# Eight input chunks loaded ahead of all weights in a scan and two-MoE kernel, with the second half's raw first-matmul blocks staged in the chunks' space

## The chip, the cores and the metric

The kernel runs as one program on 1 core of one Trainium2 chip. Its time is the device time of one execution in microseconds (us); lower is better. The engines are TensorE (PE; its weight loads are listed as PEld), VectorE (DVE), ScalarE (ACT), GpSimd (POOL) and SyncE (SP). SP does no arithmetic here: it issues transfers (DMAs). ACT and POOL issue transfers too, between their own instructions.

## The reference, cut to what matters

```python
def reference(x, f_logit, lower_bound, ...):        # x: (2, 5056, 256) f32
    f = lb + (1 - lb) * sigmoid(f_logit)
    h = 0
    for t in range(S):                               # per batch and channel
        h = f[:, t] * h + (1 - f[:, t]) * x[:, t]
        y[:, t] = h
    x = y.reshape(10112, 256)
    x = moe(x, logits = norm(x) @ norm(emb).T / tau, w1 (8,256,1024), w2 (8,1024,256))
    return moe(x, logits = x @ w_gate, another w1, w2)

def moe(x, logits, w1, w2):                          # top-1 of 8 experts
    e = argmax(logits); gate = softmax(logits)[e]
    return gate * (relu(x @ w1[e]) @ w2[e])
```

A gated scan runs over 10112 tokens (two sequences of 5056), and its output passes through two layers in which each token goes to one of eight experts.

## The kernel before, in words

**Chunks.** The scan works on chunks of 256 tokens, 40 of them, channels on the partitions. A chunk is one transfer of 512 KB (`p_load`, line 445) that holds x and the gate logits. Its steps are: `p_gate` (a tanh on ACT, line 452, and a scale and offset of two 128x256 halves on POOL, line 460, or on ACT, line 458), `p_scan` (on DVE one product, line 183, and two scans, line 486), `p_mm` (PE transposes to rows of tokens, line 501, and router logits, line 503), `p_sq`, `p_pow`, `p_hi` and `p_lo` (the rows are stored as a high and a low f16 part), and for each pair of chunks the routing (`p_seed` to `p_gat`, mostly small DVE instructions) and `p_put` (POOL scatters 128 rows at a time into the table X in DRAM, line 660).

**Weights.** Everything is multiplied in split f16: a weight block is loaded raw in f32 (`w_load`, line 370, 512 KB for one expert's half of one matrix), ACT makes its high part (`w_hi`, line 383), and the low part, raw minus high, is made either by one DVE instruction over 128x1024 (`w_lo`, line 395 through the helper at line 183) or by PE (`w_sub`, lines 404 and 405: four matmuls) with two ACT evacuations (`w_sub2`, line 413). `wpe` says how many of each 16 blocks take the way by PE: 4 of the first 16 and 8 of the second 16. Hidden features are cut in two halves h. Half 0 has 16 blocks (8 of W1, 8 of W2), and half 1 has 16 more. `W1[h]` and `W2[h]` hold the finished parts; the two tiles of half 1 also serve as space at the start:

- the first eight chunks are loaded into the eight expert slots of `W2[1]` (`alias`),
- the raw half-0 blocks of W1, then five raw half-0 blocks of W2, are loaded into the slots of `W1[1]` (`wal`); the last three go to a ring `ws` of three buffers,
- all raw half-1 blocks go through that ring.

A DVE low part of half 1 may be issued only after the first tile table is written (`issue_after(tablast[0])`, line 1144).

**Tables and units.** At checkpoints (after 16, 32, 48, 64 tiles of 128 tokens) DVE writes a table of full expert tiles (`checkpoint`, its last step `tab` at line 712). SP then reads tile addresses from it and issues a DMA transpose of each tile (`t_load`, line 767), and PE works on units: `mm1` (line 792, 24 matmuls), evacuation by ACT and DVE into `hT` (lines 800 and 801), and three units later `mm2` (lines 812 and 815). The first table gives nine tiles, 18 units: the first four tiles' half 0 (units 0 to 3), their half 1 (units 4 to 7), and then both halves of one tile after another. Unit 18 is the first that needs the second table, which needs chunks 8 to 15.

**Order.** All steps are put into numbered slots with a priority by hand (`at(slot, priority, function)`); the first unit is slot 0, and the slots run from -31. Up to slot 17 only SP's instructions keep exactly this order; the orders of PE, ACT, DVE and POOL are made by a scheduler that starts from the slots, with the steps of the first eight chunks named in `urgent` going first. `hwq()` issues a load from SP before slot -6 and from ACT afterwards. SP handles its issues strictly one after the other, so a load that waits for its space holds up all behind it.

Of the kernel before, what the change touches and what calls it, by code (L numbers as in the profile page):

```python
# [8 lines left out]
F32 = mybir.dt.float32  # L9
# [10 lines left out]
E = 8  # L20
# [9 lines left out]
 'lag': 3,  # L30
 'pre': 6,
 'start': -29,
 'wstep0': 1.2,
 'early': 4,
 'gact': (6, 16),
 'urgent': ('scan', 'mm', 'sq', 'pow', 'hi', 'seed', 'newton', 'top', 'rank', 'rec', 'exp', 'slot', 'up', 'gat', 'put', 'cp'),
 'gdve': 0,
 'wpe': (4, 8),
 'yg': (0, 0),
 'man0': ('SP',),  # L40
 'wa': 3,
# [20 lines left out]
 'spto': -6,  # L62
 'sc': (0, 26),
 'w1': (-8, 0.8),
 'w2': (0, 0.75),
 'w3': (0, 0.9),
 'wprio': 60,
# [55 lines left out]
def scan_moe_moe_kernel(ctx, tc, xf, emb, cst, tmp, w1a, w2a, w1b, w2b, out, seq, cfg=CFG):  # L123
# [53 lines left out]
    W2 = [wp.tile([P, E, 4, 2, D], F16, name=f"W2_{h}") for h in range(2)]  # L177
# [180 lines left out]
    def hwq():  # L358
        return SP if now[0] < cfg["spto"] else A
# [3 lines left out]
    def w_load(item):  # L363
        m, which, h, e = item
        k = 8 * which + e
        if (m, h) == (0, 0) and k < 8 + cfg["wal"]:
            t = W1[1][:, k % 8].rearrange("p k b f -> p (k b f)").bitcast(F32)
        else:
            t = st.tile([P, 1024], F32, name="ws", tag="ws")
        hwq().dma_start(out=t, in_=wsrc[m][which][:, h, e, :])  # L370
        return t
# [643 lines left out]
    for m in range(2):  # L1015
# [14 lines left out]
        for part in (tl, tails[m]):  # L1030
            for j in range(0, len(part), CT):
                d = dict(t=part[j:j + CT], at=j)
# [25 lines left out]
    def at(s, prio, fn, *a):  # L1058
        seqn[0] += 1
        slots.setdefault(s, []).append((prio, seqn[0], fn, a))  # L1060

    def first_of_all(fn):

        def run(*a):
            with tc.high_priority():
                r = fn(*a)
            return r and steps(r)

        def steps(r):
            while True:  # L1070
                with tc.high_priority():
                    if next(r, "end") == "end":
                        return
                yield

        return run
# [9 lines left out]
    first = min(s0.values())  # L1086
    for c in range(NCH):
        b = s0[c]
        PO = cfg["p"]

        def pa(name, fn, arg, b=b):
            if c < cfg["cps"][0] // CT and name in cfg["urgent"]:
                fn = first_of_all(fn)
            at(b + PO[name][0], PO[name][1], fn, arg)

        if c >= 2:
            pa("load", p_load, c)
        for name, fn in (("gate", p_gate), ("scan", p_scan), ("mm", p_mm), ("sq", p_sq), ("pow", p_pow), ("hi", p_hi), ("lo", p_lo)):
            pa(name, fn, c)
        if c % 2 or c == NCH - 1:  # L1100
            q = c // 2
            for name, fn in (("seed", p_seed), ("newton", p_newton), ("top", p_top), ("rank", p_rank), ("rec", p_rec), ("exp", p_exp), ("slot", p_slot),
                             ("up", p_up), ("gat", p_gat)):
                pa(name, fn, q)
            b, prio = s0[c] + PO["put"][0], PO["put"][1]
            if b < 0:
                at(b, prio, first_of_all(p_put) if c < cfg["cps"][0] // CT else p_put, q, range(G4))
            else:
                for j in range(G4):
                    at(b + j, prio, p_put, q, (j,))  # L1110

            def cp0(q):
                for m, cnt, n, fin, key in cpl:
                    if m == 0 and key not in xcnt and cnt <= min(NT, (q + 1) * G4):
                        checkpoint(m, n, fin, key, min(NT, (q + 1) * G4))

            pa("cp", cp0, q)


    def wseq(m, h):  # L1120
        return [(m, 0, h, e) for e in range(E)] + [(m, 1, h, e) for e in range(E)]
# [7 lines left out]
    def wstep(load, hi, lo, lo2):  # L1129
        def w_done(item):  # L1130
            assert item[0] or item[2] or now[0] <= 0, "weights too late"
            wdone.add(item)

        if lo2 in wps:
            w_sub2(lo2, *wps.pop(lo2))
            w_done(lo2)
        if lo is not None:
            t = wbuf.pop(lo)
            nlo[0] += 1
            i, k = nlo[0], (cfg["wpe"] + (0, 0))[(nlo[0] - 1) // 16]  # L1140
            if (i * k) // 16 != ((i - 1) * k) // 16:
                wps[lo] = (w_sub(lo, t), t)
            elif 16 < i <= 32 and tablast:
                with tc.issue_after(tablast[0]):
                    w_lo(lo, t)
                w_done(lo)
            else:
                w_lo(lo, t)
                w_done(lo)
        if hi is not None:  # L1150
            w_hi(hi, wbuf[hi])
        if load is not None:
            wbuf[load] = w_load(load)

    def wplan(items, start, step, ahead=0):
        x = start

        def it(k):
            return items[k] if 0 <= k < len(items) else None

        if ahead:
            for k in range(len(items)):
                at(max(first - 2, int(start + (k - ahead) * step)), cfg["wlp"], wstep, it(k), None, None, None)
        for k in range(len(items) + 4):
            at(int(x), cfg["wprio"], wstep, None if ahead else it(k), it(k - 2), it(k - 3), it(k - 4))
            x += step

    last_h0 = [i for i, u in enumerate(units) if u[0]["m"] == 0 and u[1] == 0][-1]
    last0 = [i for i, u in enumerate(units) if u[0]["m"] == 0 and u[0]["grp"] == 2][0]
    at(last0 + cfg["t0at"][0], cfg["t0at"][1], lambda: last_tiles(0))  # L1170
    wplan(wseq(0, 0), first + 1, cfg["wstep0"], cfg["wa"])
    wplan(wseq(0, 1), *cfg["w1"])
    wplan(wseq(1, 0), last_h0 + 1 + LAG + cfg["w2"][0], cfg["w2"][1] * cfg["swap"] / 16.0)
    wplan(wseq(1, 1), n1 + LAG + cfg["w3"][0], cfg["w3"][1] * cfg["swap"] / 16.0)

# [64 lines left out]
    def last_tiles(m):  # L1240
        tl = tails[m]
        if not tl:
            return
        n = nc.values_load(nums[m][0:1, 0:1], engines=ALL, min_val=0, max_val=TMAX)
        inside[0] = True
        if m:
            with tc.If(n > tl[0]["j"]):
                us = [(t, h) for t in tl for h in range(2)]
                for i in range(len(us) + 2):
                    if i < len(us):  # L1250
                        t, h = us[i]
                        if h == 0:
                            t_load(t, 0)
                            t_reg(t)
                        mm1(t, h)
                        evac(t, h)
                    if i >= 2:
                        t, h = us[i - 2]
                        mm2(t, h, h == 0, h == 1)
                        if h == 1:  # L1260
                            drain(s2(t))
            return
        with tc.If(n > tl[0]["j"]):
            kept[0] = {}
            assert ranked[1] == 0
            for d in [t["pair"] for t in tl if t["pi"] == 0]:
                for t in d["t"]:
                    t_load(t, 0, qp.tile([P, 8, TW], F16, name="xt8", tag="q")[:, 0:4, 0:P])
                    t_reg(t)
                    for h in range(2):  # L1270
                        mm1(t, h)
                        evac(t, h)
                        mm2(t, h, h == 0, h == 1)
                    drain(o_sum(t))
                    m_sq(t)
                for fn in (m_scale, m_split, m_turn, m_turn2, m_logits, m_top, m_exp, m_rank, m_gat, m_slot, m_up):
                    drain(fn(d))
                routed[0] += len(d["t"])
            kept[0] = None
        inside[0] = False  # L1280
# [128 lines left out]
```

## Time and profile before

| | |
|---|---|
| median of 3 runs | 1118.79 us (1114.92 to 1122.22) |
| the profiled execution: its own time | 1118.87 us |
| its span, first to last instruction | 1116.8 us |
| PE busy | 1027.6 us, 92% |
| DVE busy | 685.3 us, 61% |
| ACT busy | 534.3 us, 48% |
| POOL busy | 464.7 us, 42% |
| TensorE clock granted, mean | 0.964 of full speed |

The shares are means over the whole span, and the kernel has stages with different limits, so the section after the next shows the busy time by stretch. In a row, the name on the left of `<-` is the tile written and on the right what is read; a bracket at the end gives the idle time in front of an instruction and what ended it. `W` stands for any of the four weight tiles, so the first eight chunks appear as `W` and later ones as `xf`.

### The profile page before, as it was taken

The numbers are of one execution on the slowest core, as the hardware profiler recorded it, in microseconds if no ns is written. First come the engines' busy times: TensorE is split into PE (matmuls) and PEld (weight loads), VectorE is DVE, ScalarE is ACT, GpSimd is POOL, SyncE is SP. The second block draws the span as 40 slices with busy tenths as digits, with TensorE's granted clock in tenths as the row PEclk, the third lists the DMA queues.
The fourth block names the chain that finished last, engine by engine and source line by source line (L and its number), as shares of the span: only waits on it lengthen the run. The fifth ranks groups of instructions, "written<-read, shape, count | busy, mean of one in ns | idle before, by whom it ended". The sixth has DMA issues, their size and how long they took to land.

```text
span 1116.8 us, 33586 instructions
## 1 busy us (share of the span) xinstructions
PE 1027.6 (92%) x11987; PEld 813.1 (73%) x11987; DVE 685.3 (61%) x2227; ACT 534.3 (48%) x1338; POOL 464.7 (42%) x909
## 2 busy tenths in 40 slices
PE   3768899999999999798999889899999999999996
PEld 2435677888887887576877667687888888788885
DVE  8975687787778777454648987866433333333332
ACT  5877665555555554343436755544333333333332
POOL 4353555666666666522103665234222222222222
PEclk9777999999999999998999999899999999999999
DMA  9669535476754664222338739954222232232220
GB/s 356 229 188 243 137 87 110 121 130 127 141 121 116 135 133 84 72 62 47 68 50 212 186 84 215 223 87 97 62 50 49 54 54 49 46 56 43 44 49 28
DMA packets 191766, 124.14 MB, mean 111 GB/s; under 512 B 169345, under 2 KB 170254, under 8 KB 191600
## 3 DMA queue, kind: packets, MB, share of 16 engines
q1 hardware_dynamic: 167632, 49.15, 24.7%
q10 hardware_dynamic: 11344, 39.15, 12.9%
q0 software_dynamic: 12624, 33.62, 10.2%
q8 instruction: 105, 1.72, 0.7%
q14 instruction: 61, 0.50, 0.2%
HBM read 54.70 MB, written 34.66 MB: 80 GB/s over the span
## 4 chain that ended last, share of the span: by engine, by line
PE 44%; DVE 6%; DMA 2%; issue 1%; ACT 0%; POOL 0%; POOLq 0%; ACTq 0%
PE hps L792 22%; PE ops L812 15%; PE ops L815 7%; DVE W L183 1%; DMA ws<-w1b 1%; DVE trow L183 1%; DVE hT L183 1%; DVE trow L187 1%; DVE osum L191 1%; DMA X<-trow,tsl 1%; DVE ter L191 0%; DVE pi L188 0%; ACT W L383 0%; DVE tse L188 0%; PE x2p L901 0%
## 5 line engine op out<-in xcount | busy, mean ns | idle before, releaser
L792 PE MATMUL hps<-xT,W 128*128 128x128 f16 x7968 | 510.7, 220 | 13.1 <-issue 11.0
L792 PEld LDWEIGHTS <-W 128*128 x7968 | 477.8, 99 | 61.1 <-issue 20.5
L812 PE MATMUL ops<-W,hT 128*128 x1328 | 454.5, 382 | 9.2 <-ACT W L413 3.3
L183 DVE SCALAR_TENSOR_TENSOR hT<-hps,hT 128x512 f16<-128x512 f32 x332 | 228.4, 688 | 254.4 <-ACT hT L800 253.2
L815 PE MATMUL ops<-W,hT 128*128 x1328 | 364.3, 274 | 1.0 <-issue 1.0
L800 ACT ACTIVATE hT<-hps 128x512 f16<-128x512 f32 x332 | 197.5, 595 | 330.3 <-PE hps L792 262.1
L812 PEld LDWEIGHTS <-hT 128*128 128x128 f16 x1328 | 132.4, 100 | 124.8 <-issue 6.3
L1004 POOL DMA_INDIRECT out<-osum,ti x83 | 81.1, 977 | 290.8 <-DVE osum L183 256.1
L815 PEld LDWEIGHTS <-hT 128*128 128x128 f16 x1328 | 130.3, 98 | 19.8 <-issue 7.5
L984 POOL DMA_INDIRECT X<-trow,tsl x83 | 94.2, 1136 | 57.8 <-DVE tsl L191 31.9
L660 POOL DMA_INDIRECT X<-row,sl x79 | 85.1, 1077 | 52.7 <-issue 17.1
L833 ACT ACTIVATE ob<-ops,exr 128x256 f32<-128x256 f32 x83 | 39.3, 473 | 59.7 <-PE ops L815 52.8
L383 ACT ACTIVATE W<-ws 128x1024 f16<-128x1024 f32 x51 | 54.7, 1072 | 15.2 <-DMA ws<-w1b 7.7
L183 DVE SCALAR_TENSOR_TENSOR osum<-ops,exr,ob 128x256 f32<-128x256 f32 x83 | 40.2, 484 | 35.3 <-ACT ob L833 33.0
L183 DVE SCALAR_TENSOR_TENSOR W<-ws,W 128x1024 f16<-128x1024 f32 x42 | 51.1, 1218 | 9.4 <-ACT W L383 9.1
L191 POOL TENSOR_TENSOR ob<-ob,acc 128x256 f32<-128x256 f32 x25 | 23.2, 928 | 58.3 <-ACT ob L831 58.2
L858 ACT ACTIVATE trow<-osum 128x256 f16<-128x256 f32 x83 | 35.3, 425 | 23.8 <-DVE osum L191 14.9
L831 ACT ACTIVATE ob<-ops 128x256 f32<-128x256 f32 x83 | 31.3, 377 | 31.1 <-PE ops L815 15.0
L486 DVE TENSOR_TENSOR_SCAN xf<-xf 128x256 f32<-128x256 f32 (+3 forms) x64 | 42.6, 707 | 0.1
L191 DVE TENSOR_TENSOR osum<-ops,ob 128x256 f32<-128x256 f32 x83 | 34.5, 415 | 11.5 <-POOL ob L191 6.2
L183 DVE SCALAR_TENSOR_TENSOR trow<-osum,tsc,trow 128x256 f16<-128x256 f32 x83 | 39.1, 494 | 2.3 <-ACT trow L873 1.5
L873 ACT ACTIVATE trow<-osum,tsc 128x256 f16<-128x256 f32 x62 | 28.1, 501 | 20.9 <-DVE tsc L188 10.5
(165 smaller groups left out, 1142.8 us busy)
## 6 DMA issues: line engine op xcount, KB each, us to landing
xf<-xf ACTq DMA_DIRECT2D x28, 512.0 KB
ws<-w1b ACTq DMA_DIRECT2D x16, 512.0 KB
ws<-w2b ACTq DMA_DIRECT2D x16, 512.0 KB
W<-xf SPq DMA_DIRECT2D x8, 512.0 KB
W<-w1a SPq DMA_DIRECT2D x8, 512.0 KB
ws<-w2a ACTq DMA_DIRECT2D x8, 512.0 KB
xT<-X SPq DMA_TRANSPOSE x212
ws<-w1a ACTq DMA_DIRECT2D x6, 512.0 KB
```

The costliest lines, as they stand in the source:

```text
L183: return eng.scalar_tensor_tensor(out=out, in0=in0, scalar=s, in1=in1, op0=op0, op1=op1, **kw)
L191: return eng.tensor_tensor(out=out, in0=in0, in1=in1, op=op)
L383: A.activation(out=hi, in_=src, func=ACTF.Copy, scale=64.0)
L486: V.tensor_tensor_scan(out=t[:, k, lo:hi], data0=t[:, 2 + k, lo:hi], data1=t[:, k, lo:hi], initial=init, op0=ALU.mult, op1=ALU.subtract)
L660: x_write(0, G.indirect_dma_start(out=X[0], out_offset=IndirectOffsetOnAxis(ap=p["sl"][:, i, 0:1], axis=0), in_=p["row"][:, i, :].bitcast( ...
L792: T.matmul(out=hps[:, c, :], lhsT=w, rhs=xt[:, a, :], start=(n == 0), stop=(n == 5))
L800: A.activation(out=hh[:, 0], in_=hps, func=ACTF.Relu)
L812: T.matmul(out=o.rearrange("p a d -> p (a d)"), lhsT=hT[:, k, :], rhs=W2u[h][:, ds(at4[k], 4 * D)].bitcast(F16), start=(first and k == 0), ...
L815: T.matmul(out=o[:, 0, :], lhsT=hT[:, 4 + k, :], rhs=W2u[h][:, ds(at4[k], 2 * D)].bitcast(F16), start=False, stop=(last and k == 3))
L833: A.activation(out=b, in_=o[:, 1, :], func=ACTF.Copy, scale=scale)
L984: x_write(1, G.indirect_dma_start(out=X[1], out_offset=IndirectOffsetOnAxis(ap=sl[:, i, 0:1], axis=0), in_=d["row"][:, i].bitcast(I32), in ...
L1004: i = ins_of(G.indirect_dma_start(out=out, out_offset=IndirectOffsetOnAxis(ap=ti, axis=0), in_=r, in_offset=None, bounds_check=N - 1, oob_ ...
```

## The change

The eight chunks' loads are moved to the very first slots, the half-0 weights are planned ten slots after the first instead of one and follow at a denser step, the eight raw half-1 W1 blocks get loads of their own into the slots of `W2[1]` that the chunks leave, no half-1 block takes the way by PE, and the gate's scale and offset of chunks 4 and 5 go from POOL to ACT.

```diff
- 'wstep0': 1.2,
+ 'w0': 10,
+ 'wstep0': 0.85,
- 'gact': (6, 16),
+ 'gact': (4, 16),
- 'wpe': (4, 8),
+ 'wpe': (4, 0),
+ 'w1s': (20, 0.8),
...
+        elif (m, which, h) == (0, 0, 1):
+            t = W2[1][:, e].rearrange("p k b d -> p (k b d)").bitcast(F32)
         else:
             t = st.tile([P, 1024], F32, name="ws", tag="ws")
...
-        if c >= 2:
+        if 2 <= c < cfg["alias"]:
+            at(first - 2 + (c - 2) // 2, 2, p_load, c)
+        elif c >= 2:
             pa("load", p_load, c)
...
-    def wplan(items, start, step, ahead=0):
+    def wplan(items, start, step, ahead=0, staged=0):
...
-            at(int(x), cfg["wprio"], wstep, None if ahead else it(k), it(k - 2), it(k - 3), it(k - 4))
+            at(int(x), cfg["wprio"], wstep, None if ahead or k < staged else it(k), it(k - 2), it(k - 3), it(k - 4))
...
-    wplan(wseq(0, 0), first + 1, cfg["wstep0"], cfg["wa"])
-    wplan(wseq(0, 1), *cfg["w1"])
+    wplan(wseq(0, 0), first + cfg["w0"], cfg["wstep0"], cfg["wa"])
+    for e in range(E):
+        at(int(first + cfg["w1s"][0] + e * cfg["w1s"][1]), 60, wstep, (0, 0, 1, e), None, None, None)
+    wplan(wseq(0, 1), *cfg["w1"], staged=E)
```

Worked out from these numbers (`first` is -29): chunks 2 to 7 load in slots -31 to -29, where they were in -27 to -17. The 16 half-0 loads stand in slots -21 to -8, where they were in -31 to -13. The eight staged loads stand in slots -9 to -3, the first three on SP and the others on ACT's queue. The half-1 W2 loads keep their slots from -1 on.

## Rows read from the trace of the kernel before

**Rows 1.** Windows: busy time of each engine by stretch, clock, DMA share, GB/s.

```profile
core 0: us, PE busy (x) PEld busy (x) DVE busy (x) ACT busy (x) POOL busy (x), PEclk, DMA share, GB/s
0.00:9.00 9.00, 0.20 (x1) 0.10 (x1) 4.38 (x37) 2.17 (x3) 3.50 (x13) 1.00 0.81 257
9.00:35.00 26.00, 16.37 (x76) 12.36 (x76) 24.94 (x64) 18.93 (x48) 10.60 (x13) 1.00 0.83 323
35.00:50.00 15.00, 9.21 (x45) 5.99 (x46) 15.00 (x58) 15.00 (x42) 5.83 (x5) 0.66 0.83 301
50.00:62.00 12.00, 11.64 (x44) 6.43 (x43) 10.71 (x52) 9.64 (x26) 6.24 (x6) 0.57 0.44 147
62.00:73.60 11.60, 6.31 (x48) 4.33 (x45) 8.57 (x52) 8.83 (x33) 5.41 (x9) 0.87 0.81 236
73.60:89.00 15.40, 10.07 (x22) 4.59 (x21) 10.97 (x26) 9.17 (x22) 5.45 (x17) 0.61 0.78 190
89.00:109.00 20.00, 16.52 (x141) 12.30 (x139) 10.22 (x23) 14.12 (x30) 8.75 (x22) 0.78 0.97 253
109.00:135.00 26.00, 22.69 (x190) 15.31 (x189) 17.32 (x42) 17.04 (x45) 15.72 (x31) 0.93 0.70 166
135.00:157.70 22.70, 20.41 (x229) 16.34 (x228) 18.50 (x73) 13.65 (x44) 14.95 (x41) 1.00 0.28 84
...
157.70:1116.80 959.10, 914.14 (x11211) 735.36 (x11208) 564.69 (x1812) 425.71 (x1057) 388.21 (x757) 0.98 0.45 94
```

**Rows 2.** Timeline: the first and second table's last step, first and nineteenth unit.

```profile
73.39 0.23 DVE L188 TENSOR_SCALAR tab<-le,ct 128x9 int32<-128x9 f32 x1
...
157.53 0.22 DVE L188 TENSOR_SCALAR tab<-le,ct 128x16 int32<-128x16 f32 x1
...
89.04 1.91 PE L792 MATMUL hps<-xT,W 128*128 128x128 f16 x16
...
158.56 1.22 SPq L767 DMA_TRANSPOSE xT<-X  x1
...
169.21 1.50 PE L792 MATMUL hps<-xT,W 128*128 128x128 f16 x24
```

**Rows 3.** Timeline of SP's issues, and the longest wait of SP before 60 us.

```profile
18.42 13.47 SPq L370 DMA_DIRECT2D W<-w2a  x2
31.95 0.42 SPq L445 DMA_DIRECT2D W<-xf  x1
...
34.56 0.95 SPq L445 DMA_DIRECT2D xf<-xf  x2
...
SPq L370 <- PE wd L404: 12.8, 1, 12.8
```

**Rows 4.** Timeline of ACT: the tanh of chunks 0, 7 and 8.

```profile
5.52 0.63 ACT L452 ACTIVATE W<-W 128x512 f32<-128x512 f32 x1 [2.49 <-DMA W<-xf]
...
41.50 0.77 ACT L452 ACTIVATE W<-W 128x512 f32<-128x512 f32 x1
...
49.28 0.82 ACT L452 ACTIVATE xf<-xf 128x512 f32<-128x512 f32 x1
```

**Rows 5.** DVE groups by shape, 50 to 73.6 us: work of chunks 8 and later.

```profile
L183 DVE SCALAR_TENSOR_TENSOR row<-yt,sc,row 128x256 f16<-128x256 f32 x8 | 3.7, 473 | 0.4 <-ACT row L541 0.4
L486 DVE TENSOR_TENSOR_SCAN xf<-xf 128x256 f32<-128x256 f32 x4 | 2.9, 740 | 0.0
...
L183 DVE SCALAR_TENSOR_TENSOR xf<-xf 128x512 f32<-128x512 f32 x3 | 2.1, 702 | 0.1
L486 DVE TENSOR_TENSOR_SCAN xf<-xf,W 128x256 f32<-128x256 f32 x2 | 1.4, 733 | 0.0
```

**Rows 6.** DVE groups by shape, 73.6 to 157.7 us: weight low parts.

```profile
L183 DVE SCALAR_TENSOR_TENSOR W<-ws,W 128x1024 f16<-128x1024 f32 x8 | 9.7, 1219 | 4.9 <-ACT W L383 4.9
```

**Rows 7.** What DVE waited for from 73.6 to 157.7 us: total, times, longest.

```profile
DVE hT L183 <- ACT hT L800: 8.1, 6, 3.6
DVE ri L615 <- POOL ri L188: 5.1, 3, 3.2
DVE W L183 <- ACT W L383: 4.9, 4, 2.1
DVE xf L183 <- ACT xf L458: 4.2, 2, 3.0
DVE ci L183 <- PE ops L815: 1.6, 1, 1.6
```

**Rows 8.** PE groups by shape, 73.6 to 157.7 us: the way by PE.

```profile
L404 PE MATMUL wd<-ws,cs 128*128 128x512 f32 x28 | 20.4, 850 | 6.6 <-DMA ws<-w1a 6.6
...
L405 PE MATMUL wd<-W,idn 128*128 128x512 f16 x14 | 5.5, 446 | 0.0
```

**Rows 9.** ACT and POOL groups by shape: 9 to 62, 73.6 to 157.7, 0 to 62 us.

```profile
L458 ACT ACTIVATE W<-W,fb,fa 128x256 f32<-128x256 f32 x4 | 2.4, 704 | 0.0
...
L383 ACT ACTIVATE W<-ws 128x1024 f16<-128x1024 f32 x13 | 14.0, 1080 | 7.5 <-DMA ws<-w2a 4.7 <-DMA ws<-w1a 2.8
...
L413 ACT ACTIVATE W<-wd 128x512 f16<-128x512 f32 x14 | 7.9, 597 | 2.5 <-POOL rq L188 2.2 <-DVE ri L615 0.4
...
L188 POOL TENSOR_SCALAR W<-W,fa,fb 128x256 f32<-128x256 f32 x12 | 11.3, 949 | 16.6 <-ACT W L452 16.6
```

## The prediction, made before the changed kernel was run

> **What bounds the kernel now.** I read the windows first, because the shares of the whole span hide the start. From 157.7 us on PE is busy 914 of 959 us, 95% [rows 1]. The change touches no step of that part, so whatever comes earlier there moves the end by as much, and nothing else does. The lever is the head, in which PE is busy 113 of 157.7 us, part of it with weight preparation.
>
> The head has two stretches. From 9 to 50 us DVE is busy 39.9 of 41 us, 97%, while PE stands at 62% [rows 1]: DVE is the bound. From 73.6 to 157.7 us, between the two tables, DVE is busy 57.0 of 84.1 us (10.97 + 10.22 + 17.32 + 18.50), 68%; PE is busy 69.7, 83%, at a granted clock of 0.61 to 0.93 up to 135 us; ACT 54.0, 64% [rows 1]. No engine is full there; each waits for another in turn.
>
> The next view is the timeline of the tables and units. The first table ends at 73.6, the first unit starts at 89.0, the second table ends at 157.75, SP issues the transpose of unit 18 at 158.56, and PE takes that unit at 169.2 without an idle gap [rows 2]. The first unit came 15.4 us after its table, and the nineteenth came 11.5 us after its own. So PE has little slack over the second table: I estimate that it could run some 5 us ahead, and after that the second table decides. The date to forecast is that of the second table.
>
> Last, SP's own timeline. It stands in one wait of 12.8 us for a PE weight subtraction, from 18.4 to 31.6 us, since a raw W2 block wants a slot that a raw W1 block still occupies; chunk 7's load is queued behind it and issues at 31.95 [rows 3]. Chunk 0's tanh runs at 5.52, chunk 7's at 41.5 and chunk 8's at 49.3 [rows 4]. The first table needs chunk 7.
>
> **The change part by part.**
>
> Chunks first: chunks 2 to 7 are issued before any load that waits. At 323 GB/s, the rate of 9 to 35 us [rows 1], 512 KB take 1.6 us, so chunk 7 lands near 5.5 + 7 x 1.6 = 17 us, and no chunk step waits for a load. What is late next is DVE itself. Its work up to the first table was 4.38 + 24.94 + 15.00 + 10.71 + 8.57 = 63.6 us [rows 1]. Of this about 10 us belongs to chunks 8 to 10 and was only filler: scans 2.9 + 1.4, products 2.1, half of the eight row parts 1.9 [rows 5], and an estimated 1.7 of small routing steps. The other 53.6 stay: eight chunks, twelve half-0 low parts, setup, table. With 4.4 of it done by 9 us and the 97% of 9 to 50 us, taken as 96%, the table ends at 9 + 49.2 / 0.96 = 60.3 us instead of 73.6: **13.3 us earlier**. Bounds: if the scheduler puts all twelve half-0 low parts (12 x 1.22 = 14.6 us, by the mean of [rows 6]) behind the table it comes at 45, but that work then stands in the second stretch; if the order of the urgent steps stays as it is and the table still waits for its chain of small steps, it comes at 70.
>
> Half-0 weights later: eight W1 blocks of 1.6 us land behind the chunks, from 17 to about 30 us, before DVE has time for them. Nothing is lost while DVE is full. The raw W2 blocks still need the slots that these leave, so SP waits again, but now only chunks 8 and later, the W2 blocks and the three first staged loads stand behind that wait. Chunk 8's load issued at 34.56 before [rows 3] and could come 10 to 15 us later; at no cost as long as low parts fill DVE, and at up to that much idle time of DVE if they don't.
>
> Staged half-1 W1 blocks: the eight loads leave the ring of three. ACT waited 2.8 us for such blocks and 4.7 for the W2 ones [rows 9], PE 6.6 [rows 8], and DVE stood 4.9 us behind ACT's high parts [rows 7]. A staged slot is free only when its chunk's scan and transposes are over and the next chunk's scan has read its last column; for slot 7 that is chunk 8's scan. Five of the loads are issued by ACT, so ACT's evacuations and tanhs are queued behind such a wait if the order turns out wrong; I take nothing for it, and 3 us as its upper bound, the order of the single waits that these rows show.
>
> No half-1 block by PE: in the second stretch PE loses 20.4 + 5.5 = 25.9 us of busy time [rows 8] and ACT 7.9 us of evacuations [rows 9]. DVE gains eight low parts, 8 x 1.219 = 9.75 us [rows 6], all behind the first table. PE is not the bound of the table, so its 25.9 us are not a term of their own; they show in how long DVE waits.
>
> Gates of chunks 4 and 5: four POOL instructions, 4 x 0.95 = 3.8 us, become four on ACT, 4 x 0.70 = 2.8 us [rows 9]. ACT is full from 35 to 50 us [rows 1], but it loses the wait for chunk 7 and a first table at 60 leaves it slack: its 54.6 us up to 73.6 included later chunks as well. Zero, between a 2.8 us loss and, since POOL's step was in the chain of its chunk, a 1 us gain.
>
> **The sum.** Work of DVE between the tables: 57.0, plus 10 of chunks 8 to 10 that no longer stand in front of the first table, plus 9.75, minus an estimated 5.5 for scans and row parts of chunks 16 and 17 that ran before the second table without being needed: 71.2 us. Idle time of DVE there was 84.1 - 57.0 = 27.1 us. Of its causes [rows 7] the 5.1 us for POOL's small steps and 1.6 for the table's start stay. The 4.9 behind high parts should go, and the 8.1 for hT and 4.2 for gates are in part PE and ACT being held by the subtractions. There is also 20 us more work to stand in the holes. I take half, 13.5 us. The second table then ends at 60.3 + 71.2 + 13.5 = 145.0 us, 12.7 us earlier. PE can follow: it needs some 26 us less for the same units. The profiled execution took 1118.87 us, 0.1 us from the median of the runs, so 1118.87 - 12.7 = **1106 us**.
>
> The low parts go to the engine that is fullest in the head. The Trainium skill, Perfetto Trace Analysis, section Identifying the Most-Contended Engine, tells one to find the engine with the highest occupancy and to optimize it first; this edit loads that engine. By that page alone, with DVE the bound of the whole head, the time would grow. The trace agrees for 9 to 50 us and not behind the first table, where the new low parts stand. The rival it gives is the third below.
>
> **The rivals.**
>
> 1. More. If low parts and chunks keep DVE as full behind the first table as before it (7 us idle instead of 13.5) and the table comes some us earlier still, the second table ends at 60.3 + 71.2 + 7 = 138.5, 19 us earlier: 1100 us, down to 1094. For it: the work is loaded long before. Against: 5.1 + 1.6 us of waits stay, and PE and ACT get the units' work at the same time.
>
> 2. Hidden. DVE's idle time between the tables stays at 22 to 27 us, because each hT, gate and routing step still waits for another engine in turn; the earlier first table is eaten by the moved work. 60.3 + 71.2 + 22 = 153.5 gives 4 us, 27 gives 158.5: 1114 to 1120 us. For it: no engine was full in that stretch, and the total work of DVE up to the second table rises.
>
> 3. Slower, with DVE as the bound. The first table does not come earlier by what the loads allow, because DVE's chain of small steps at the end of the routing sets it and the low parts are put among them; then the 9.75 us of added low parts stand on DVE between the tables with nothing to pay for them. Second table at 157.75 + 9.75 = 167.5: 1128.6 us. It decides from the point where DVE's share between the tables falls under 71.2 / (157.75 - 60.3) = 73%, or where the first table comes later than 73.6 - 9.75 + 5.5 = 69 us with idle time as it is. For it: DVE is 97% full up to 50 us. Against: 27 us of holes behind the first table.
>
> That the change doesn't do what it says is possible only on the engines whose order the scheduler makes; it would show as rival 2.
>
> **How the numbers follow.** Forecast, 1100 to 1112: 0.45. Rival 1, below 1100: 0.15. Rival 2, 1112 to 1122: 0.25. Rival 3, above 1122: 0.15. A change of 1% is 11.2 us, about what a measurement of this kernel can tell from none, so faster means below 1107.6 and slower above 1130. Faster: all of rival 1 and some three quarters of the forecast's weight, 0.48. Slower: the upper part of rival 3, 0.10. The rest, 0.42, is within 1%. The likeliest case alone spans 1100 to 1112; the range for 8 in 10 cuts half of rival 1 and most of rival 3: 1096 to 1124.
>
> **What would show it.** SP's timeline should have chunk 7's issue before 10 us and no wait in front of it. The tanh of chunk 7 should stand before 35 us, the first table's last step near 60, the first unit near 70 to 75. Behind it, there should be 16 low parts of 1.2 us on DVE, no line 404 with half-1 blocks, and ACT's waits for raw W1 blocks gone. The second table should stand near 145 and unit 18 some 10 us behind it. From there on the distance to the end should be as before, 959 us from the second table. The prediction is wrong if the second table moves much less than the first, if ACT stalls at its staged loads, or if the part behind the second table changes its length.

## The result, and the profile after

The changed kernel takes 1110.21 us (median of 11 runs, 1107.01 to 1116.94) against 1118.79 us for the kernel before on the same chip (11 runs, 1114.92 to 1122.61): a ratio of 0.9914, 95% interval 0.989 to 0.9939. The profiled execution took 1111.67 us, its span 1109.4. The gain is 8.6 us; 12.7 were predicted, and the time lies 4.2 us above the predicted 1106.

The first view is again that of the windows, now cut at the two tables and the first unit (columns as in [rows 1]):

```profile
core 0: us, PE busy (x) PEld busy (x) DVE busy (x) ACT busy (x) POOL busy (x), PEclk, DMA share, GB/s
0.00:9.00 9.00, 0.20 (x1) 0.10 (x1) 4.20 (x36) 1.91 (x2) 3.51 (x13) 1.00 0.79 266
9.00:50.00 41.00, 27.30 (x134) 22.32 (x135) 39.76 (x139) 35.29 (x97) 12.59 (x13) 1.00 0.75 269
50.00:60.00 10.00, 3.86 (x14) 1.96 (x14) 9.04 (x57) 7.75 (x13) 6.40 (x7) 0.66 1.02 395
60.00:86.30 26.30, 13.76 (x63) 9.59 (x62) 22.48 (x43) 20.84 (x46) 17.53 (x23) 0.63 0.92 294
86.30:109.00 22.70, 18.76 (x199) 16.97 (x199) 19.53 (x51) 18.97 (x51) 13.88 (x25) 0.83 0.93 222
109.00:135.00 26.00, 22.52 (x217) 16.76 (x217) 16.11 (x52) 10.77 (x39) 18.61 (x41) 0.87 0.35 89
135.00:149.60 14.60, 11.45 (x138) 9.20 (x137) 12.56 (x60) 9.20 (x29) 8.80 (x26) 1.00 0.19 65
149.60:1109.40 959.80, 914.88 (x11184) 734.51 (x11181) 561.81 (x1805) 425.28 (x1053) 389.57 (x762) 0.98 0.45 95
```

Up to the first table DVE works 4.20 + 39.76 + 9.04 = 53.0 us. Between the tables it works 22.48 + 19.53 + 16.11 + 12.56 = 70.7 of 89.6 us, so it is idle for 18.9. Behind the second table the kernel takes 959.8 us and PE is busy 914.9 of them; before, 959.1 and 914.1 [rows 1].

The timeline of the changed kernel, with the rows that answer to [rows 2 to 4] (tanh of chunks 7 and 8; tables; first unit and units 17 and 18; SP):

```profile
21.94 0.66 ACT L456 ACTIVATE W<-W 128x512 f32<-128x512 f32 x1
53.07 0.63 ACT L456 ACTIVATE xf<-xf 128x512 f32<-128x512 f32 x1
...
59.70 0.22 DVE L190 TENSOR_SCALAR tab<-le,ct 128x9 int32<-128x9 f32 x1
149.36 0.22 DVE L190 TENSOR_SCALAR tab<-le,ct 128x16 int32<-128x16 f32 x1
...
86.33 4.90 PE L796 MATMUL hps<-xT,W 128*128 128x128 f16 x48
...
161.62 1.50 PE L796 MATMUL hps<-xT,W 128*128 128x128 f16 x24
164.31 1.50 PE L796 MATMUL hps<-xT,W 128*128 128x128 f16 x24
...
2.13 4.55 SPq L449 DMA_DIRECT2D W<-xf  x7
6.73 9.72 SPq L374 DMA_DIRECT2D W<-w1a  x8
30.48 17.19 SPq L374 DMA_DIRECT2D W<-w2a  x4
47.72 0.42 SPq L449 DMA_DIRECT2D xf<-xf  x1
...
79.31 1.30 SPq L771 DMA_TRANSPOSE xT<-X  x1
...
154.97 1.22 SPq L771 DMA_TRANSPOSE xT<-X  x1
```

The reader is to see four dates. Chunks 1 to 7 issue by 6.7 us, chunk 7's tanh runs at 21.9 instead of 41.5 [rows 4], and the first table ends at 59.9 instead of 73.6 [rows 2]. The first unit came only 2.7 us earlier, 86.3 instead of 89.0. The second table ends at 149.6, 8.2 us earlier. SP's wait moved: it stands from 16.5 to 30.5 us, and again up to 47.7, with the raw W2 blocks, and chunk 8's load, behind them, issues 13.2 us later than in [rows 3]:

```profile
SPq L374 <- PE RK L429: 11.8, 1, 11.8
SPq L374 <- DVE lg L193: 10.8, 1, 10.8
```

A count in [rows 2] is off by one. The row at 169.21 there is not the nineteenth unit; 17 evacuations into hT run on ACT before it, so it is unit 17, the eighteenth. Unit 18 follows it, in the trace of the kernel before:

```profile
171.90 1.50 PE L792 MATMUL hps<-xT,W 128*128 128x128 f16 x24
```

So unit 18 began at 171.90 before and begins at 164.31 now, 13.3 and 9.3 us behind SP's transpose for it, with no idle time of PE in front in either trace. The slack of PE over the second table was larger than the estimated 5 us.

The groups of DVE by shape from 60 us to the second table, which answer to [rows 6, 7]:

```profile
L185 DVE SCALAR_TENSOR_TENSOR W<-ws,W 128x1024 f16<-128x1024 f32 x9 | 10.8, 1214 | 0.0
L185 DVE SCALAR_TENSOR_TENSOR hT<-hps,hT 128x512 f16<-128x512 f32 x14 | 9.5, 682 | 10.3 <-ACT hT L804 8.6 <-issue 1.7
L185 DVE SCALAR_TENSOR_TENSOR W<-W,W 128x1024 f16<-128x1024 f32 x8 | 9.5, 1212 | 2.0 <-ACT W L387 2.0
```

And its waits in the same stretch:

```profile
DVE hT L185 <- ACT hT L804: 8.6, 3, 5.2
DVE xf L185 <- ACT xf L462: 2.2, 2, 1.4
DVE W L185 <- ACT W L387: 2.0, 2, 1.8
...
DVE ri L619 <- POOL ri L190: 0.5, 1, 0.5
```

Seventeen low parts stand behind the first table (the sixteen of half 1 and the last of half 0). The wait behind high parts fell from 4.9 to 2.0 us, POOL's small steps from 5.1 to 0.5. The wait for hT, 8.1 us before, stands at 8.6, of which 5.2 is one wait.

### The profile page after: what moved, and what is told of

It is laid out like the page before. It is cut to its first block, busy times and chain, and to the rows that moved or that the text cites. A ratio compares the mean times of both kernels' runs of the same rounds, so it can differ in the third digit from the quotient of the medians.

```text
span 1109.4 us, 33481 instructions
## 1 busy us (share of the span) xinstructions
PE 1012.7 (91%) x11939; PEld 811.4 (73%) x11939; DVE 685.5 (62%) x2235; ACT 530.0 (48%) x1326; POOL 470.9 (42%) x905
## 4 chain that ended last, share of the span: by engine, by line
PE 46%; DVE 5%; DMA 2%; issue 1%; ACT 1%; another core or an unknown queue 0%; POOL 0%; ACTq 0%; POOLq 0%; DVEq 0%
PE hps L796 23%; PE ops L816 15%; PE ops L819 8%; DVE W L185 2%; DMA ws<-w1b 1%; DVE hT L185 1%; DMA X<-trow,tsl 1%; PE x2p L905 1%; ACT W L387 0%; DVE osum L193 0%; DVE trow L185 0%; DVE ter L193 0%; DVE trow L189 0%; DVE acc L193 0%
## 5 line engine op out<-in xcount | busy, mean ns | idle before, releaser
L664 POOL DMA_INDIRECT X<-row,sl x79 | 91.3, 1155 | 57.2 <-ACT lg L525 23.3
L387 ACT ACTIVATE W<-ws 128x1024 f16<-128x1024 f32 x43 | 45.4, 1058 | 6.2 <-DMA ws<-w1b 5.1
L505 PE MATMUL yt<-cs,xf 128*128 128x128 f32 x126 | 28.5, 303 | 19.7 <-issue 9.2
L835 ACT ACTIVATE ob<-ops 128x256 f32<-128x256 f32 x83 | 31.4, 378 | 30.7 <-PE ops L819 15.0
```

The lines of the kernel that those rows point to most:

```text
L387: A.activation(out=hi, in_=src, func=ACTF.Copy, scale=64.0)
L664: x_write(0, G.indirect_dma_start(out=X[0], out_offset=IndirectOffsetOnAxis(ap=p["sl"][:, i, 0:1], axis=0), in_=p["row"][:, i, :].bitcast( ...
```

## The experiments

Three theories stood against each other: the order of the loads carries the gain, through the first table (A); the work that PE loses carries it (B, called D in the later expectations); the loads that no longer wait for the ring of three carry it (C). The change has three large parts, here called **order** (of the loads), **staging** (of the half-1 W1 blocks) and **low parts** (all of half 1 on DVE). The runs below hold all eight combinations. They ran on two chips, numbered 0 (the first eight runs) and 11 (the last three); each ratio is to the kernel before on its own chip (medians there 1095.05 to 1098.12 us). The result's chip has no number on record; it is taken for a third, because the kernel before took 1118.8 us on it. The times in the first four expectations are for that chip, so they are to be read as ratios to 1118.8 us.

**Order and staging, low parts left out.** The change with the second half's eight blocks back on PE.

```diff
- 'wpe': (4, 0),
+ 'wpe': (4, 8),
```

> The changed kernel with the second half's low parts shared as before: 8 of 16 by PE. Theory A (the head ends with the second table, which DVE's work and its holes set; the load order brought the first table forward): first table near 60 us as in the changed kernel, DVE between the tables loses 9.75 us of work and regains about as much in holes while PE gets 26 us back; second table 147 to 153, total 1107 to 1114. Theory B (the gain is the 26 us that PE lost; the load order is idle): second table back near 157, total 1117 to 1120.

Measured: 1090.32 us, 0.9956 (0.9924 to 0.9987). First table 59.2, second 150.9, first unit 90.1. The table dates and the ratio lie within what theory A had, the ratio at its upper edge.

**Order and low parts, staging left out.** The half-1 W1 blocks go through the ring again.

```diff
-        elif (m, which, h) == (0, 0, 1):
-            t = W2[1][:, e].rearrange("p k b d -> p (k b d)").bitcast(F32)
...
-    for e in range(E):
-        at(int(first + cfg["w1s"][0] + e * cfg["w1s"][1]), 60, wstep, (0, 0, 1, e), None, None, None)
-    wplan(wseq(0, 1), *cfg["w1"], staged=E)
+    wplan(wseq(0, 1), *cfg["w1"], staged=0)
```

> The changed kernel with the raw half-1 W1 blocks through the ring of three again instead of the chunks' slots. Theory A: first table near 60, but ACT's high parts of these blocks wait for the ring; second table 152 to 156, total 1112 to 1117. Rival (the staging is idle, since low parts may start only behind the first table and DVE has a queue anyway): 1108 to 1112.

Measured: 1090.26 us, 0.9955 (0.9933 to 0.9976). First table 58.9, second 151.7, first unit 81.3. The staging is not idle here: without it the ratio lies above that of the change (0.9846, below), with intervals apart.

**Order alone.** The kernel before with the new order of loads. Against the changed kernel it has both edits above together, and the gates of chunks 4 and 5 on POOL.

```diff
- 'gact': (4, 16),
+ 'gact': (6, 16),
- 'wpe': (4, 0),
+ 'wpe': (4, 8),
...
+    wplan(wseq(0, 1), *cfg["w1"], staged=0)
```

> Only the load order of the change (chunks first, half-0 weights later); ring, 8 of 16 by PE and the gates of chunks 4 and 5 on POOL as before. Theory A: first table 58 to 64, second table 150 to 156, total 1111 to 1117. Theory B: the first table comes early but the second stays near 157, total 1117 to 1120.

Measured: 1099.49 us, 1.003 (1.0001 to 1.0059). Theory A fell here: the first table came at 61.2, some 12 us early, and nothing was gained. The second table came at 167.0, later than either theory had it.

**Low parts alone.** The kernel before with one number changed.

```diff
- 'wpe': (4, 8),
+ 'wpe': (4, 0),
```

> The kernel before with all half-1 low parts on DVE, nothing else. Theory A: first table stays near 73, 9.75 us more work on DVE stand in 27 us of holes; second table 156 to 164, total 1117 to 1125. Theory B: PE's 26 us are the gain, second table near 149, total 1108 to 1112.

Measured: 1086.78 us, 0.9923 (0.9896 to 0.9949), as theory B had it. The second table came at 152.2. It is the largest single part, though it puts an estimated 9.75 us more (eight low parts of [rows 6]) on DVE, the fullest engine of the head.

**The change itself**, on the chip of these runs.

> The changed kernel itself, as the measure for the others on this chip: ratio to the kernel before 0.988 to 0.994, second table 8 us earlier than before.

Measured: 1080.0 us, 0.9846 (0.9806 to 0.9885), a larger gain than expected. First table 60.2, second 145.0.

**Staging alone.** The kernel before with the staged loads (the two blocks of code above, added to it).

> The kernel before with the raw half-1 W1 blocks staged in the chunks' slots, nothing else (old load order, 8 of 16 by PE). Theory C (the head's end is set by the half-1 blocks' way through the ring of three, where a block that PE takes holds its slot until PE has read it): ratio 0.990 to 0.996, second table near 151. Theory D (PE's 26 us of subtractions are what counts): ratio 0.998 to 1.003, second table near 157.

Measured: 1093.89 us, 0.9985 (0.9958 to 1.0011): not told from no change. Second table 154.0. Theory C by itself fell.

**Staging and low parts, old order.**

```diff
# the kernel before with the staged loads, and
- 'wpe': (4, 8),
+ 'wpe': (4, 0),
```

> The kernel before with staging and all half-1 low parts on DVE, but the old load order and gates. Theory A (load order carries the gain): ratio near 0.997 to 1.0. Theory C with an idle load order: 0.986 to 0.993, as good as the whole change or better by the 0.3% that the order alone lost. Theory D: the 0.992 of low parts on DVE alone.

Measured: 1089.5 us, 0.9944 (0.9926 to 0.9962), between the ranges of theories A and C; the 0.992 of theory D lies just under the interval. Without the order some 9.5 us of the gain are gone, though the order alone is worth nothing. (Its profiled execution took 1099.39 us, 10 above its median.)

**Chunks 8 and 9 earlier.** Their loads go ahead of the half-0 weights, to test whether SP's wait in front of chunk 8 costs.

```diff
+        elif 8 <= c < 10:
+            at(first + 6, 2, p_load, c)
```

> The changed kernel with the loads of chunks 8 and 9 moved ahead of the raw half-0 blocks, so that they no longer stand behind SP's 17 us wait. If DVE is full up to the first table and the late chunk 8 costs nothing: ratio to the changed kernel 0.998 to 1.002. If the late chunks make the holes behind the first table: second table 3 to 5 us earlier, ratio 0.995 to 0.997.

Measured: 1085.85 us, 0.9926 (0.9896 to 0.9955), some 6 us worse than the change, which neither expectation had. Chunk 8's tanh ran at 24.2 instead of 53, and the first table came at 64.7 and the first unit at 91.3: DVE and ACT did chunk 8's work in front of the table that doesn't need it.

**The kernel before**, for its trace on a second chip.

> The kernel before, unchanged, for its trace on this chip. If its shorter time here (1095 to 1096 us against 1118.8) lies behind the second table, as the changed kernel's traces of both chips let one think (959.8 against 937 us), then its second table stands at 155 to 160 us as in the first trace and the distance to the end is near 935. If the head is what differs, the second table comes before 145 and the distance is 950 or more.

Measured: 1096.74 us. Second table at 160.2, 934.6 us ahead of the end, so the shorter time of this chip lies behind the second table.

**Gates left on POOL.**

```diff
- 'gact': (4, 16),
+ 'gact': (6, 16),
```

> The change without its last part: the gates of chunks 4 and 5 stay on POOL. My prediction took this part as 0, between a loss of 2.8 us and a gain of 1: then the time is within 0.3% of the changed kernel's 1080.0 us (ratio to the kernel before 0.982 to 0.988), first table at 59 to 62. The rival: in the orders tried so far the load order and the gates went together or not by turns, and the gates carry what I gave to the interplay of the three edits; then this kernel falls back to a ratio of 0.993 to 0.997, as the kernels with one of the three edits missing did.

Measured: 1082.64 us, 0.9863 (0.9832 to 0.9895): inside the band for "no part". The gates of chunks 4 and 5 are worth nothing that shows, and the run without order, e3, is not spoiled by its gates.

**The change once more**, for a second trace.

> The changed kernel once more, for a second trace on one chip. If the 4.6 us between the second tables of its two traces (149.6 and 145.0) come from the chip, this one shows 144 to 146. If a profiled execution scatters by as much, it can stand anywhere from 143 to 151, and my term for the idle time of DVE can't be called off by 5 us.

Measured: 1082.67 us; second table 144.8. That is as on chip 0 (145.0), and not as on the result's (149.6), which speaks for the chip as the cause; from the result's chip there is one trace.

### What the eight combinations show together

Units run on PE in one order, so a date up to which the kernels can be compared is the end of unit 17's matmuls, where its evacuation starts. It splits into the start of the first unit and the stretch from there. The ratio is of all runs, the dates are of one profiled execution each (us). The first line's trace is from chip 11, the other seven from chip 0:

| parts | ratio | first unit | stretch to unit 17 | PE busy, idle in it | unit 17 done |
|---|---|---|---|---|---|
| none | 1 | 90.4 | 83.2 | 70.8, 12.4 | 173.6 |
| order | 1.003 | 93.0 | 87.4 | 71.2, 16.2 | 180.4 |
| staging | 0.9985 | 90.8 | 76.7 | 70.4, 6.3 | 167.5 |
| low parts | 0.9923 | 83.3 | 82.3 | 67.0, 15.3 | 165.6 |
| order, staging | 0.9956 | 90.1 | 74.2 | 68.6, 5.6 | 164.3 |
| order, low parts | 0.9955 | 81.3 | 83.8 | 65.1, 18.7 | 165.1 |
| staging, low parts | 0.9944 | 93.3 | 74.5 | 64.9, 9.6 | 167.8 |
| all three | 0.9846 | 85.8 | 70.7 | 61.6, 9.1 | 156.5 |

These dates do not add up to the ratios. From unit 17 to the end the eight traces have 916.6 to 929.8 us, though no part touches that stretch. Staging alone is 6.1 us earlier at unit 17 and gains 0.15%, some 1.6 us, by the medians. The change without its gates, as fast as the change, has its first unit at 89.5 and unit 17 at 161.0. So the ratios show which parts work together, and the dates only suggest by which way.

Each line comes from a windows view cut at those two dates. Here are those on which the reading rests, each kernel's line up to the first unit and from there. The kernel before, on the second chip:

```profile
0.00:90.40 90.40, 52.07 (x228) 33.26 (x229) 74.59 (x280) 64.03 (x164) 37.86 (x60) 0.79 0.74 249
90.40:173.60 83.20, 70.84 (x730) 53.26 (x729) 57.10 (x181) 53.88 (x143) 43.31 (x103) 0.92 0.61 148
```

Low parts alone:

```profile
0.00:83.30 83.30, 39.52 (x201) 27.28 (x201) 72.05 (x270) 59.32 (x153) 37.75 (x59) 0.77 0.73 259
83.30:165.60 82.30, 67.03 (x707) 56.06 (x708) 65.08 (x201) 50.07 (x139) 46.34 (x104) 0.84 0.69 162
```

Staging and low parts, old order:

```profile
0.00:93.30 93.30, 42.76 (x202) 29.08 (x202) 79.82 (x274) 65.15 (x158) 44.45 (x59) 0.74 0.77 274
93.30:167.80 74.50, 64.89 (x707) 54.90 (x708) 55.68 (x195) 44.08 (x134) 44.15 (x104) 0.87 0.47 121
```

Order and low parts, no staging:

```profile
0.00:81.30 81.30, 43.23 (x212) 32.92 (x213) 67.76 (x263) 58.09 (x150) 36.83 (x56) 0.88 0.73 256
81.30:165.10 83.80, 65.05 (x698) 53.20 (x699) 68.41 (x207) 53.83 (x148) 50.69 (x104) 0.85 0.63 168
```

The change, second trace:

```profile
0.00:85.70 85.70, 45.92 (x212) 33.96 (x213) 75.86 (x271) 66.53 (x159) 39.44 (x55) 0.86 0.84 288
85.70:155.90 70.20, 61.39 (x698) 50.40 (x699) 56.37 (x199) 45.47 (x136) 46.64 (x105) 0.95 0.54 139
```

Three readings follow. The first two are read from traces; the third rests on the ratios.

**Low parts on DVE free the way to the first unit.** In front of it PE's busy time falls from 52.1 to 39.5 us, and the unit comes 7.1 us earlier. The work that went is PE's own, in a stretch where its granted clock is 0.61 [rows 1]. The kernel before, on the result's chip, shows it between the first table and the first unit:

```profile
L404 PE MATMUL wd<-ws,cs 128*128 128x512 f32 x8 | 7.5, 1094 | 3.1 <-DMA ws<-w1a 3.1
...
L405 PE MATMUL wd<-W,idn 128*128 128x512 f16 x2 | 1.1, 634 | 0.0
```

That is 8.6 us of subtractions and 3.1 us of waiting for raw blocks, out of 15.4 us; the others of the same kind follow among the units. What stands just in front of the first unit differs too. In the kernel before it is a subtraction up to 89.0, and with the low parts alone it is an idle PE that waits for the transposed tile:

```profile
85.49 3.75 PE L404 MATMUL wd<-ws,cs 128*128 128x512 f32 x4 [1.23 <-DMA ws<-w1a]
...
83.33 2.08 PE L792 MATMUL hps<-xT,W 128*128 128x128 f16 x18 [2.21 <-DMA xT<-X]
```

SP issued the first transpose at 77.5 us in the one and at 77.4 in the other, so if the tile took as long to land in both, PE's own order held the unit by 5.7 us.

**Staging moves half-1 low parts from behind the first unit to ahead of it.** The windows say so: with all low parts on DVE in both, DVE's work ahead of the first unit rises from 72.0 to 79.8 us under the old order and from 67.8 to 75.9 under the new one, and in the unit stretch it falls from 65.1 to 55.7 and from 68.4 to 56.4. In low parts that is 16 without staging against 23 with it that are done before the first unit under the old order, and 15 against 22 under the new. The unit stretch gets shorter by 7.8 us under the old order and by 13.1 or 13.6 (two traces of the change) under the new one.

**The order pays for staging.** By the ratios staging is worth something on the new order alone: from 1.003 to 0.9956 without the low parts and from 0.9955 to 0.9846 with them, both with intervals apart. On the old order it gives -0.15% without the low parts and 0.2% of loss with them, neither told from nothing. How that comes about is argued from the dates. Under the old order the first unit comes 10.0 us later for that work (83.3 to 93.3, the latter in the execution that took 10 us above its median), and nothing is left of the 7.8. Under the new order the first table, and with it the chunks' part of DVE's work, is 13 us earlier, and the first unit is only 4.5 us later (81.3 to 85.8), 8.2 in the trace without the gates. The order alone has no low parts to put into that room: the half-0 weights stand later, the last weight part is finished at 146.9 instead of 139.9, and the units wait (16.2 us of idle PE against 12.4). So the single parts add up to 0.003 - 0.0015 - 0.0077, or -0.6%, and together they give -1.5%.

A larger ring, which would tell the position of the loads from the space they take, was not tried. And the dates are of one execution each, with no interval of their own.

## Why the prediction was right, and where it was off

The result is in the range and nearest to the forecast's case, 1.8 us from the edge where the second rival begins. The single likeliest outcome by the chances, faster by 1% or more (0.48), did not come; 0.86% falls within 1% (0.42). Of the prediction's signs of being wrong, the first came half true: the second table moved by 8.2 us, the first by 13.7. The others did not come: the one wait of ACT for a staged block took 2.0 us, and the part behind the second table kept its length. By the steps:

**First table**: 60.3 predicted, 59.9 measured, with 53.0 us of DVE work against 53.6. The 96% held.

**Work between the tables**: 71.2 predicted, 70.7 measured.

**Idle time between the tables**: this is the mis-sized term. "I take half, 13.5 us" met 18.9 on the result's chip, 5.4 more; with the 0.9 us that the first two terms gave back, it makes all of the miss, 149.6 instead of 145.0. By its causes it was off in both directions: the 5.1 us for POOL's small steps, which were to stay, fell to 0.5, and the 8.1 for hT, which were to go in part, stood at 8.6. The other two traces of the changed kernel have 85.0 - 71.0 = 14.0 and 84.8 - 70.2 = 14.6 us. The windows and waits of the second:

```profile
60.00:144.80 84.80, 63.97 (x610) 50.18 (x609) 70.22 (x202) 60.67 (x164) 55.59 (x112) 0.85 0.69 191
```

```profile
DVE osum L193 <- POOL ob L193: 3.4, 1, 3.4
DVE W L185 <- ACT W L387: 2.9, 2, 2.3
DVE xf L185 <- POOL xf L190: 2.7, 1, 2.7
...
DVE hT L185 <- ACT hT L804: 0.3, 1, 0.3
```

The wait for hT is 0.3 us there and 8.6 in the result's trace; an hT waits for PE to reach its unit. On the result's chip PE had a granted clock of 0.87 from 109 to 135 us and did 217 matmuls. That is a mean over both levels: from 117 to 121 us it was at 1.00 with PE busy for 2.86 of the 4 us, and from 121 to 125 us at 0.57. In this trace it had 1.00, the upper level (2.4 GHz), throughout and did 250 in the same busy time (22.5 and 22.4 us):

```profile
109.00:135.00 26.00, 22.44 (x250) 18.22 (x251) 18.16 (x63) 14.60 (x50) 20.19 (x47) 1.00 0.42 124
```

The third trace of the changed kernel has 0.93 there, 250 matmuls and a wait for hT of 1.1 us. Why the clock differs is not settled, and that it makes the wait is argued from these three traces; there is one of the changed kernel from the result's chip.

**Distance to the end**: "as before, 959 us" and 959.8 measured.

**"PE is not the bound of the table, so its 25.9 us are not a term of their own."** The first half of this sentence failed, and the sum survived it. The low parts alone are half of the change's worth on their chip, and they work through PE: the first unit 7.1 us earlier. The second half held: between the tables of that run DVE is idle for 17.1 us, against 29.2 in the kernel before on chip 11, and the second table comes 8.0 us earlier. In the result's own traces the gain up to unit 17 can be written wholly in PE's terms. Before, and then after:

```profile
89.00:170.80 81.80, 72.73 (x730) 54.87 (x729) 55.92 (x181) 53.21 (x144) 43.50 (x103) 0.92 0.60 150
```

```profile
86.30:163.20 76.90, 64.51 (x698) 52.43 (x699) 56.86 (x199) 45.67 (x140) 48.39 (x105) 0.90 0.51 125
```

The first unit is 2.7 us earlier, PE works 8.2 us less in the stretch and idles 3.3 more (12.4 for 9.1): 2.7 + 8.2 - 3.3 = 7.6 us, against 7.2 in the two profiled executions. That is a way to book the gain and not yet a proof of its cause. The second table served as a mark, since PE's order mixes the units with the chunks' transposes and logits that the table needs; it was not what unit 18 waited for. The prediction took it for the cause, and that its distance to the end stayed the same was in this sense luck. As a mark it is as good as unit 17: from the second table to the end the eleven traces of chips 0 and 11 have 930.0 to 941.3 us, from unit 17 916.6 to 929.8.

**"Half-0 weights later: nothing is lost while DVE is full."** Not so by itself: the order alone finishes its weights 7 us later and is slower by 0.3%. In the change staging and the low parts on DVE finish all weights at 109 us, and there the order gains 1.0% (0.9944 to 0.9846).

**Staging.** It was priced by the waits of ACT, PE and DVE for raw blocks (at most 4.9 + 2.8 + 4.7 + 6.6). Those fell: ACT's from 7.5 us [rows 9] to 2.4, not to zero. What the runs suggest as its worth is another thing: seven more low parts done ahead of the first unit, where the new order had made room.

**Chunk 8 later.** Foreseen as 10 to 15 us, measured 13.2. No cost of it was found: bringing it forward made the kernel slower.

**Gates.** Taken as zero; the change without them differs by less than its interval.

**First unit near 70 to 75.** Wrong: 86.3. The sixteen scatters of the first eight chunks end at 74.0, hardly ahead of the 75.6 before, because POOL's first one waits for the routing until 40.7 and two of them are slow (below); the first transpose follows at 79.3. But in the other two traces the transposes began at 73.1 and 76.6 and the first unit still came at 85.8 and 85.7. In front of it on PE stand the transposes and logits of chunks behind the table, at a clock of 0.63 from 60 to 86.3 us in the result's trace, and waits for DVE and ACT. Which of them holds it was not separated.

**The rivals.** The third needed DVE to be the bound between the tables. The run with the low parts alone is its direct test, some 9.75 us more on DVE, and it is 0.77% faster. The Trainium skill, Perfetto Trace Analysis, section Identifying the Most-Contended Engine, says to find the engine with the highest occupancy and optimize it first. In the stretch in question this trace has PE, not DVE, as the fuller engine by the time of its matmuls (83% against 68% [rows 1]), and so taken the rule agrees with the result; by the whole head it does not. But for TensorE the same section of the Trainium skill sets the matmul time aside as a measure and names, beside the arithmetic done, the busy share of the weight loads. That share is 48.5 of 84.1 us here, 58% [rows 1], less than DVE's, and so taken the rule misses the result in this stretch too.

The second rival, idle time of 22 us or more, did not come true, though 18.9 lies nearer to it than to the forecast's 13.5; the first (7 us) came true in no trace.

## What to carry to other kernels

Room that a new load order makes early in a kernel is worth nothing until other work is ready to be put into it: the order alone gave nothing (+0.3%) and staging alone nothing (-0.15%), but both together gave -0.4%, and with the lightened PE (-0.8% alone) -1.5%. So parts of a change are to be priced together where one makes room and another fills it. And a date that moves with the end is not yet its cause: before pricing by it, look at whether the instruction behind it had idle time in front.

## What the runs showed of the hardware that was not expected

**The time differs by the chip.** The same kernel before takes 1118.8 us on the result's chip and 1095 to 1098 on chips 0 and 11. Its trace from chip 11 has 934.6 us behind the second table against 959.1 [rows 1]:

```profile
160.20:1094.80 934.60, 903.15 (x11217) 731.65 (x11214) 566.38 (x1812) 430.11 (x1058) 388.27 (x755) 0.99 0.46 97
```

PE is busy for 903.2 against 914.1 us at a mean clock of 0.99 against 0.98, and idle for 31.4 against 45.0. The gain differs as well (0.9914, and 0.9846 with an interval that doesn't reach it), so a ratio of one chip is not exact for another.

**Two scatters take four times as long.** A scatter on POOL takes 0.97 to 1.44 us from 54 us to the first table's last one in the kernel before. In the changed kernel two of them take 3.82 and 4.38 us:

```profile
59.67 0.97 POOL L664 DMA_INDIRECT X<-row,sl  x1 [0.30 <-issue]
60.95 3.82 POOL L664 DMA_INDIRECT X<-row,sl  x1 [0.30 <-DMA X<-row,sl]
65.07 4.38 POOL L664 DMA_INDIRECT X<-row,sl  x1 [0.30 <-issue]
69.76 1.12 POOL L664 DMA_INDIRECT X<-row,sl  x1 [0.30 <-ACT lg L525]
```

The DMA share is 1.00 from 60 to 70 us, but a full share alone doesn't explain them. It is 1.02 from 50 to 60 us in the same trace, and the seven scatters that start there take 0.97 to 1.11 us. In the other two traces of the changed kernel the scatter near 61 us takes 3.82 us as well, and the next one 0.98 and 2.12.

The Trainium skill, DMA: Bandwidth & Descriptors, section Issuing engines are not separate DMA queues, says that transfers started by the scalar, sync or gpsimd engine run on the same 16 DMA engines and interleave. By that the loads that SP and ACT start could lengthen POOL's scatters, but no run here shows it, and the cause stays open.
